# Retention and two MLPs on one core: act_b later in its step, first loads of gl and wos earlier, four p buffers, other stores and accumulators

## The chip, the core and the metric

The kernel runs on one core of a Trainium2 chip. The metric is the device time of one execution in microseconds (us). TensorE (PE) multiplies, with its weight loads shown apart as PEld; VectorE (DVE), ScalarE (ACT) and GpSimd (POOL) do the elementwise work, and SyncE (SP) issues nearly all DMA transfers. Each engine works through its own instructions in the order in which the program wrote them (the pool's scheduler is off: `manual_schedule`), and waits where an operand or a buffer isn't ready.

## The reference

Eight batches of eight heads, 576 positions, 64 wide, go through retention with one decay per head; the result, as 4608 tokens of 512, goes through two MLPs of width 2048.

```
scores = q @ k.T / 8                       # per batch and head
ret    = scores * where(i >= j, gamma[h] ** (i - j), 0)
x      = (ret @ v), laid out as tokens x 512
h = x @ w_in;   g = h * sigmoid(1.702 * h);   x = g @ w_out      # first MLP
h = x @ w_in2;  g = h - tanh(h);              out = g @ w_out2   # second MLP
```

The weights arrive as float64, seen as int64.

## The kernel before

Every operand of the large matmuls is kept as a sum of two parts, a rounded one and the rest, and a product takes three matmuls (`PASS`: 0,0; 0,1; 1,0).

**Blocks and steps.** The tokens are cut into 9 blocks of 512; the first MLP has blocks j = 0 to 8, the second j = 9 to 17, and each block has 16 steps f, one for each 128 columns of the hidden width. Step s = 16 j + f. `mm_in(s)` (L387) makes h, 12 matmuls into a PSUM tile of the pool `ps_h` (two buffers). `act_a(s)` makes t = activation(h): in the first MLP one operation on ACT (L396) and one on DVE (L397); in the second three on ACT (L401 to L403) and a chain of five on DVE (L404, L406 to L409). `g_store` (L413) writes t to DRAM.

**The lag.** The output matmuls run `LAG` = 32 steps behind: in step s the group o = s - 32. `wo_load` (L179, tile wos, three buffers, 512 KB) and `g_load` (L417, tile gl, two buffers, 256 KB) fetch weights and t for group o + 2. `act_b(o + 1)` splits gl into the two halves of g: ACT copies it (L422), DVE subtracts (L423). `mm_out(o)` (L439 where j < 9, with g as the moving side; L441 from j = 9 on, with g as the weights) adds 12 matmuls, three for each of four accumulators. After 16 groups `evac` copies the accumulators out: in the first MLP ACT into tiles o of the pool p (L449; three buffers, shared with the attention's tile p) and SP to DRAM (L450), in the second into one tile (L457, in the last block DVE's L455 too) and to the output (L459).

**What else stands in a step.** Until step 126 every second step holds an attention step (`attn_step`: L243, L257, L272, L308 on PE; L280 to L294 and L323 on DVE; L322 and L330 on ACT). The weights are decoded from float64 in 64 chunks, three pieces each (`dec_piece`: dec_a and dec_a2, dec_b, dec_c and dec_d, L104 to L140): a load stg by SP (L96), six operations on DVE and two on ACT. At the end of dec_d (L140) the 48 chunks that are not needed at once are stored to DRAM as wd (L143). Ten steps from s = 32 on hold three pieces, the later ones two. In four steps (f = 6, 8, 10, 12) of blocks j = 8 to 16 `x2_split` prepares the next block of the second MLP: ACT copies (L471), POOL subtracts (L472).

**The order in a step from s = 32 on** is the code's: mm_in(s), act_b(o + 1), attention, a decode piece, act_a(s), loads for o + 2, g_store(s - 1), mm_out(o), more decode pieces, evac at f = 15, x2_split. The first two pairs of loads and act_b(0) are issued in step 32 itself. Steps 288 to 319 hold only the output side; in the last block the accumulators are the two halves of `pat`, the attention's PSUM tile, and two tiles of `ps_h`.

Of the kernel before, what the change touches and what calls it, by code (L numbers as in the profile page):

```python
# [7 lines left out]
F32 = mybir.dt.float32  # L8
# [8 lines left out]
P = 128  # L17
# [6 lines left out]
BLK = 512  # L24
NB = NT // BLK
KD = DM // P
NF = DFF // P
# [13 lines left out]
LAG = 2 * NF  # L41
# [5 lines left out]
def kernel(  # L47
# [14 lines left out]
    wos_p = ctx.enter_context(tc.tile_pool(name="wos", bufs=3))  # L62
    x_p = ctx.enter_context(tc.tile_pool(name="x", bufs=3))
    at_p = ctx.enter_context(tc.tile_pool(name="at", bufs=2))
    p_p = ctx.enter_context(tc.tile_pool(name="p", bufs=3))
    g_p = ctx.enter_context(tc.tile_pool(name="g", bufs=2))
    t_p = ctx.enter_context(tc.tile_pool(name="t", bufs=2))
    st_p = ctx.enter_context(tc.tile_pool(name="st", bufs=2))
# [2 lines left out]
    ps_h = ctx.enter_context(tc.tile_pool(name="ps_h", bufs=2, space=bass.MemoryType.PSUM))  # L71
# [18 lines left out]
    wo_d = {}  # L90
    stg = {}
    half = {}

    def wload(m, f, c):
        t = st_p.tile([P, BLK], I64, tag="stg", name="stg", bufs=3)
# [42 lines left out]
    def dec_d(m, f, c):  # L138
        o, sv = half.pop((m, f, c))
        nc.vector.tensor_tensor(out=sv[:, 1], in0=o, in1=sv[:, 0].bitcast(F32), op=ALU.subtract)  # L140
        if (m, c) != (0, 0):
            d = dram.tile([P, 2 * DM], F32, tag=f"w{m}{f}{c}", name="wd")
            nc.sync.dma_start(out=d, in_=sv.rearrange("p a n -> p (a n)").bitcast(F32))  # L143
            (wo_d if c else w2_d)[m, f] = d
# [10 lines left out]
    def dec_piece(pieces=1):  # L155

        for _ in range(pieces):
            n, k = divmod(n_dec[0], 3)
            if n >= len(chunks) + 2:
                return  # L160
            n_dec[0] += 1
            if k == 0:
                dec_load(n + 2)
                if n >= 2:
                    dec_c(*chunks[n - 2])
                if 1 <= n <= len(chunks):
                    dec_b(*chunks[n - 1])
                continue
            if k == 1 and n >= 2:
                dec_d(*chunks[n - 2])  # L170
            if n < len(chunks):
                (dec_a if k == 1 else dec_a2)(*chunks[n])

    def wo_load(o):
        j, f = divmod(o, NF)
        if j >= 2 * NB - 2:
            return
        t = wos[o] = wos_p.tile([P, 2, DM], F32R, tag="wos", name="wos")
        nc.sync.dma_start(out=t.rearrange("p a n -> p (a n)").bitcast(F32), in_=wo_d[int(j >= NB), f])  # L179
# [43 lines left out]
    pat = ps_a.tile([P, 2, BLK], F32, name="pat")  # L223
# [148 lines left out]
    gl = {}  # L372
    gt = {}
    acc = {}
# [17 lines left out]
    def act_a(s):  # L392
        h = hps.pop(s)
        tt[s] = t = t_p.tile([P, BLK], F32, tag="t", name="t", bufs=3)
        if s < NB * NF:
            nc.scalar.activation(out=t, in_=h, func=ACTF.Tanh, scale=0.851)  # L396
            nc.vector.scalar_tensor_tensor(out=t, in0=t, scalar=1.0, in1=h, op0=ALU.add, op1=ALU.mult)  # L397
            return
        sq = t_p.tile([P, BLK], F32, tag="e", name="sq")
        pl = t_p.tile([P, BLK], F32, tag="z", name="pl", bufs=3)  # L400
        nc.scalar.activation(out=t, in_=h, func=ACTF.Tanh)  # L401
        nc.scalar.activation(out=sq, in_=h, func=ACTF.Square)  # L402
        nc.scalar.activation(out=pl, in_=sq, func=ACTF.Square, bias=abias)  # L403
        nc.vector.tensor_tensor(out=t, in0=h, in1=t, op=ALU.subtract)  # L404

        nc.vector.scalar_tensor_tensor(out=pl, in0=pl, scalar=CB, in1=sq, op0=ALU.add, op1=ALU.mult)  # L406
        nc.vector.scalar_tensor_tensor(out=pl, in0=pl, scalar=C2, in1=h, op0=ALU.mult, op1=ALU.mult)  # L407
        nc.vector.tensor_scalar(sq.bitcast(I32), sq, S_MAX, None, ALU.is_lt)
        nc.vector.copy_predicated(out=t, mask=sq.bitcast(I32), data=pl)  # L409

    def g_store(s):
        gd[s] = dram.tile([P, BLK], F32, tag=f"g{s % (LAG + NF)}", name="gd")
        nc.sync.dma_start(out=gd[s], in_=tt.pop(s))  # L413

    def g_load(s):
        t = gl[s] = t_p.tile([P, BLK], F32, tag="gl", name="gl")
        nc.sync.dma_start(out=t, in_=gd.pop(s))  # L417

    def act_b(s):
        t = gl.pop(s)  # L420
        gt[s] = g = g_p.tile([P, 2, BLK], F32R, tag="g", name="g")
        nc.scalar.activation(out=g[:, 0], in_=t, func=ACTF.Copy)  # L422
        nc.vector.tensor_tensor(out=g[:, 1], in0=t, in1=g[:, 0].bitcast(F32), op=ALU.subtract)  # L423

    def mm_out(s):
        j, f = divmod(s, NF)
        if f == 0:
            for m in range(4):
                if j < 2 * NB - 1:
                    acc[m] = ps_acc.tile([P, BLK], F32, tag=f"acc{m}", name=f"acc{m}")  # L430
                else:
                    acc[m] = pat[:, m] if m < 2 else ps_h.tile([P, BLK], F32, tag="h", name="acc")
        g, wo = gt.pop(s), wos.pop(s)
        for m in range(4):
            c = slice(m * P, (m + 1) * P)
            for n, (a, b) in enumerate(PASS):
                first, last = f == 0 and n == 0, f == NF - 1 and n == 2
                if j < NB:
                    nc.tensor.matmul(acc[m], lhsT=wo[:, a, c], rhs=g[:, b], start=first, stop=last)  # L439
                else:  # L440
                    nc.tensor.matmul(acc[m], lhsT=g[:, a, c], rhs=wo[:, b], start=first, stop=last)  # L441
# [50 lines left out]
    with tc.tile_pool(name="ps_e", bufs=RING - 1, space=bass.MemoryType.PSUM) as ps_e:  # L492

        def early(b):
            attn_early(b, ps_e.tile([P, 2, BLK], F32, tag="e", name="pe") if b % RING else pat)


        warm = g_p.tile([P, BLK], BF16, tag="g", name="warm")
        nc.gpsimd.memset(warm, 0.0)
        for _ in range(N_WARM):  # L500
            nc.tensor.matmul(pat[:, 1], lhsT=warm[:, 0:P], rhs=warm, start=True, stop=True)

        for b in range(BPB + 1):
            if b < BPT:
                for hp in (2 * b, 2 * b + 1):
                    at_scale(0, hp)
                for i in range(2):
                    for k in range(2):
                        h = 2 * (2 * b + k) + i
                        nc.scalar.activation(  # L510
                            out=mt_sb[:, b, i, k], in_=mk_sb, func=ACTF.Copy, scale=jt_sb[:, h:h + 1]
                        )
            early(b)
            dec_piece(int(b > 0))

        for f in range(NF):
            mm_in(f)
            if f < NF // 2:
                dec_piece(3)
                act_a(f)  # L520
                early(BPB + 1 + f)
            else:
                s = NF + 2 * (f - NF // 2)
                g_store(s - 1 if f > NF // 2 else f - 1)
                mm_in(s)
                dec_piece(2)
                act_a(f)
                early(BPB + 1 + f)
                dec_piece()
                act_a(s)  # L530
                g_store(f)
                mm_in(s + 1)
                dec_piece(2)
                act_a(s + 1)
                g_store(s)
            if 0 < f < NF // 2:
                g_store(f - 1)
    ps_acc = ctx.enter_context(tc.tile_pool(name="ps_acc", bufs=1, space=bass.MemoryType.PSUM))

    n_steps = 2 * NB * NF  # L540
    for s in range(LAG, n_steps + LAG):
        j, f = divmod(s, NF)
        o = s - LAG
        if o == 0:
            g_store(s - 1)
            for i in range(2):
                wo_load(i)
                g_load(i)
            act_b(0)
        if s < n_steps:  # L550
            mm_in(s)
        if s < n_steps + LAG - 1:
            act_b(o + 1)
        if s % 2 == 0 and EARLY + (s - LAG) // 2 <= TILES * BPT:
            attn_step(EARLY + (s - LAG) // 2)
        dec_piece()
        if s < n_steps:
            act_a(s)
        if s < n_steps + LAG - 2:
            wo_load(o + 2)  # L560
            g_load(o + 2)
        if o and s <= n_steps:
            g_store(s - 1)
        mm_out(o)
        dec_piece(2 if j == 2 and f < 10 else 1)
        if f == NF - 1:
            evac(o)
        if NB - 1 <= j < 2 * NB - 1:
            if f == 2:
                x2_load(j - NB + 1)  # L570
            if f in (6, 8, 10, 12):
                x2_split(j - NB + 1, (f - 6) // 2)
        if j == NB - 1:
            w2_load(f)
        if j == 2 * NB - 1:
            wo_stay(f)
# [54 lines left out]
```

## Time and profile before

| | us |
|---|---|
| median of 3 runs (lowest, highest) | 1811.34 (1808.97, 1815.0) |
| the profiled execution | 1809.77 |
| its span, first to last instruction | 1808.0 |
| PE busy in it | 1752.8 |
| DVE, ACT, POOL busy | 1070.4, 711.9, 132.7 |

The mean granted clock of PE is 0.987 of full. The profile's lines name the source line, the engine, the operation and the tiles (out<-in, buffer numbers left out); a bracket at a line's end gives the idle time ahead of it and what ended it. In the chain of waits each piece is what released the next. Matmuls are pipelined, so a row's length for several of them is a little more than the time to the next group.

### The profile page before, as it was taken

The numbers are of one execution on the slowest core, as the hardware profiler recorded it, in microseconds if no ns is written. First come the engines' busy times: TensorE is split into PE (matmuls) and PEld (weight loads), VectorE is DVE, ScalarE is ACT, GpSimd is POOL, SyncE is SP. The second block draws the span as 40 slices with busy tenths as digits, with TensorE's granted clock in tenths as the row PEclk, the third lists the DMA queues.
The fourth block names the chain that finished last, engine by engine and source line by source line (L and its number), as shares of the span: only waits on it lengthen the run. The fifth ranks groups of instructions, "written<-read, shape, count | busy, mean of one in ns | idle before, by whom it ended". The sixth has DMA issues, their size and how long they took to land.

```text
span 1808.0 us, 24474 instructions
## 1 busy us (share of the span) xinstructions
PE 1752.8 (97%) x8908; PEld 1424.1 (79%) x8908; DVE 1070.4 (59%) x1810; ACT 711.9 (39%) x1307; POOL 132.7 (7%) x111
## 2 busy tenths in 40 slices
PE   8899898999999999999999999999999999999998
PEld 5667776877778888888888888888888888888877
DVE  7887674656555333232247767767776767776622
ACT  3433333333333232222234454454445445454422
POOL 3211010101000001100000000101010100000000
PEclk9999998999999999999999999999999999999999
DMA  5656897987888666657985756575657575658733
GB/s 218 220 196 240 297 334 265 317 277 282 294 284 301 236 212 223 234 183 243 302 296 195 245 195 235 195 247 187 238 199 239 188 246 195 234 205 303 264 123 100
DMA packets 158377, 428.76 MB, mean 237 GB/s; under 512 B 17968, under 2 KB 18096, under 8 KB 152624
## 3 DMA queue, kind: packets, MB, share of 16 engines
q1 hardware_dynamic: 157680, 427.10, 69.3%
q8 instruction: 71, 1.16, 0.3%
q14 instruction: 50, 0.41, 0.1%
q10 hardware_dynamic: 576, 0.08, 0.0%
HBM read 307.57 MB, written 119.54 MB: 236 GB/s over the span
## 4 chain that ended last, share of the span: by engine, by line
PE 79%; DMA 8%; DVE 7%; ACT 2%; issue 2%; SPq 1%; ACTq 0%; DVEq 0%
PE h L387 36%; PE acc L441 20%; PE acc L439 18%; DMA gl<-gd 7%; PE pat L441 1%; PE pat L257 1%; DVE t L397 1%; DVE p L280 1%; PE pat L308 1%; DVE e L120 1%; DVE ws L140 1%; PE pat L243 1%; SPq L179 1%; ACT g L422 1%; DMA x<-o 1%
## 5 line engine op out<-in xcount | busy, mean ns | idle before, releaser
L387 PE MATMUL h<-xh,wi 128*128 128x512 f32 x2304 | 763.4, 393 | 15.0 <-DVE t L397 8.6
L387 PEld LDWEIGHTS h<-xh,wi 128*128 128x128 f32 x2304 | 434.5, 189 | 117.8 <-DVE t L397 15.9
L439 PE MATMUL acc<-g,wos 128*128 128x512 f32 x1728 | 433.1, 399 | 25.3 <-ACT o L449 15.1
L387 PE MATMUL h<-xl,wi 128*128 128x512 f32 x1152 | 450.3, 391 | 0.0
L423 DVE TENSOR_TENSOR g<-gl,g 128x512 fp32r<-128x512 f32 x288 | 198.4, 689 | 392.3 <-ACT g L422 392.1
L439 PEld LDWEIGHTS acc<-g,wos 128*128 128x128 f32 x1728 | 324.9, 191 | 104.8 <-ACT o L449 17.0
L422 ACT ACTIVATE g<-gl 128x512 fp32r<-128x512 f32 x288 | 181.9, 632 | 508.5 <-DMA gl<-gd 324.4
L441 PE MATMUL acc<-wos,g 128*128 128x512 f32 x1344 | 322.8, 389 | 0.0
L441 PEld LDWEIGHTS acc<-wos,g 128*128 128x128 f32 x1344 | 252.2, 188 | 52.4
L387 PEld LDWEIGHTS h<-xl,wi 128*128 128x128 f32 x1152 | 217.6, 189 | 44.4
L404 DVE TENSOR_TENSOR t<-h,t 128x512 f32<-128x512 f32 x144 | 99.7, 693 | 193.8 <-ACT sq L402 193.4
L401 ACT ACTIVATE t<-h 128x512 f32<-128x512 f32 x144 | 86.0, 598 | 254.6 <-PE h L387 254.5
L397 DVE SCALAR_TENSOR_TENSOR t<-t,h 128x512 f32<-128x512 f32 x144 | 98.3, 683 | 62.0 <-ACT t L396 61.8
L108 ACT ACTIVATE e<-e,ebias 128x512 int32<-128x512 int32 x64 | 46.4, 725 | 170.8 <-DVE e L106 170.8
L409 DVE COPY_PREDICATED t<-sq,pl 128x512 f32<-128x512 int32 x144 | 109.3, 759 | 4.9
L403 ACT ACTIVATE pl<-sq,abias 128x512 f32<-128x512 f32 x144 | 104.2, 724 | 4.7
L406 DVE SCALAR_TENSOR_TENSOR pl<-pl,sq 128x512 f32<-128x512 f32 x144 | 99.7, 692 | 9.2
L472 POOL TENSOR_TENSOR xl<-x2s,xh 128x512 fp32r<-128x512 f32 x36 | 46.6, 1296 | 774.1 <-ACT xh L471 774.1
L407 DVE SCALAR_TENSOR_TENSOR pl<-pl,h 128x512 f32<-128x512 f32 x144 | 98.9, 687 | 4.9
L396 ACT ACTIVATE t<-h 128x512 f32<-128x512 f32 x144 | 84.4, 586 | 37.3 <-PE h L387 36.7
L215 POOL TENSOR_TENSOR at<-at,qt_sb 128x512 f32<-128x512 f32 x35 | 46.8, 1337 | 694.8 <-DMA at<-in_attn_dram 582.8
L402 ACT ACTIVATE sq<-h 128x512 f32<-128x512 f32 x144 | 85.4, 593 | 0.0
(62 smaller groups left out, 1121.2 us busy)
## 6 DMA issues: line engine op xcount, KB each, us to landing
wos<-wd SPq DMA_DIRECT2D x256, 512.0 KB, 4.5
gd<-t SPq DMA_DIRECT2D x288, 256.0 KB, 4.4
gl<-gd SPq DMA_DIRECT2D x288, 256.0 KB, 4.4
at<-in_attn_dram SPq DMA_DIRECT2D x35, 1024.0 KB, 5.8
stg<-in_w_dram SPq DMA_DIRECT2D x64, 512.0 KB, 6.4
wd<-ws SPq DMA_DIRECT2D x48, 512.0 KB, 3.6
x<-o SPq DMA_DIRECT2D x36, 256.0 KB, 2.8
x2s<-x SPq DMA_DIRECT2D x9, 1024.0 KB, 5.7
```

The costliest lines, as they stand in the source:

```text
L387: nc.tensor.matmul(h, lhsT=win[f][:, a, k], rhs=xs[b][:, k], start=(n == 0), stop=(n == 3 * KD - 1))
L397: nc.vector.scalar_tensor_tensor(out=t, in0=t, scalar=1.0, in1=h, op0=ALU.add, op1=ALU.mult)
L401: nc.scalar.activation(out=t, in_=h, func=ACTF.Tanh)
L403: nc.scalar.activation(out=pl, in_=sq, func=ACTF.Square, bias=abias)
L404: nc.vector.tensor_tensor(out=t, in0=h, in1=t, op=ALU.subtract)
L406: nc.vector.scalar_tensor_tensor(out=pl, in0=pl, scalar=CB, in1=sq, op0=ALU.add, op1=ALU.mult)
L407: nc.vector.scalar_tensor_tensor(out=pl, in0=pl, scalar=C2, in1=h, op0=ALU.mult, op1=ALU.mult)
L409: nc.vector.copy_predicated(out=t, mask=sq.bitcast(I32), data=pl)
L422: nc.scalar.activation(out=g[:, 0], in_=t, func=ACTF.Copy)
L423: nc.vector.tensor_tensor(out=g[:, 1], in0=t, in1=g[:, 0].bitcast(F32), op=ALU.subtract)
L439: nc.tensor.matmul(acc[m], lhsT=wo[:, a, c], rhs=g[:, b], start=first, stop=last)
L441: nc.tensor.matmul(acc[m], lhsT=g[:, a, c], rhs=wo[:, b], start=first, stop=last)
```

## The change

Six edits: the pool p has four buffers; gl has three; dec_d no longer stores wd itself, but leaves it to `dec_store`, which the third decode piece of a chunk calls before its own work; the first two pairs of wo_load and g_load stand in the last two rounds of the early part and not in step 32; act_b(o + 1) stands behind act_a(s) and not ahead of the attention; and the accumulators of the last two blocks are other ones: block 16 takes the halves of `pat` for m = 0 and 1, block 17 the ordinary tiles for m = 0 and 1 and `ps_h` for the other two.

```
@@ pools @@
-    p_p = ctx.enter_context(tc.tile_pool(name="p", bufs=3))
+    p_p = ctx.enter_context(tc.tile_pool(name="p", bufs=4))
...
+    part = {}
@@ dec_d, dec_store @@
         if (m, c) != (0, 0):
+            part[m, f, c] = sv
+
+    def dec_store():
+        while part:
+            (m, f, c), sv = part.popitem()
             d = dram.tile([P, 2 * DM], F32, tag=f"w{m}{f}{c}", name="wd")
             nc.sync.dma_start(out=d, in_=sv.rearrange("p a n -> p (a n)").bitcast(F32))
             (wo_d if c else w2_d)[m, f] = d
@@ dec_piece @@
             n, k = divmod(n_dec[0], 3)
+            if k == 2:
+                dec_store()
@@ g_load @@
-        t = gl[s] = t_p.tile([P, BLK], F32, tag="gl", name="gl")
+        t = gl[s] = t_p.tile([P, BLK], F32, tag="gl", name="gl", bufs=3)
@@ mm_out @@
-                if j < 2 * NB - 1:
+                if j == 2 * NB - 2 and m < 2:
+                    acc[m] = pat[:, m]
+                elif j == 2 * NB - 1 and m > 1:
+                    acc[m] = ps_h.tile([P, BLK], F32, tag="h", name="acc")
+                else:
                     acc[m] = ps_acc.tile([P, BLK], F32, tag=f"acc{m}", name=f"acc{m}")
-                else:
-                    acc[m] = pat[:, m] if m < 2 else ps_h.tile([P, BLK], F32, tag="h", name="acc")
@@ early part, f >= 8 @@
                 g_store(s)
+                if f >= NF - 2:
+                    wo_load(f - NF + 2)
+                    g_load(f - NF + 2)
@@ steps from 32 on @@
             g_store(s - 1)
-            for i in range(2):
-                wo_load(i)
-                g_load(i)
             act_b(0)
         if s < n_steps:
             mm_in(s)
-        if s < n_steps + LAG - 1:
-            act_b(o + 1)
         if s % 2 == 0 and EARLY + (s - LAG) // 2 <= TILES * BPT:
             attn_step(EARLY + (s - LAG) // 2)
         dec_piece()
         if s < n_steps:
             act_a(s)
+        if s < n_steps + LAG - 1:
+            act_b(o + 1)
```

In the changed kernel the lines have other numbers: act_b's copy is L430, act_a's L404 (first MLP) and L409 to L411 (second), x2_split's copy L481, the attention's L330 and L338, the decode's L109 and L136, the loads L187 and L425, the stores L149 and L421.

**ACT, two steps of the first MLP with attention in the first of them.** The names: g<-gl is act_b, xh<-pat and sbd0 are the attention, e and ws the decode, t<-h is act_a. Before:

```order
L422 ACTIVATE g_3375<-gl_3345 128x512
L322 ACTIVATE xh_2701<-pat_104 128x2x128
L330 ACTIVATE sbd0_100<-s_sb0_102 64x2x64 x2
L135 ACTIVATE ws_3402<-z_3244 128x512
L396 ACTIVATE t_3406<-h_3362 128x512
L108 ACTIVATE e_3430<-e_3430,ebias_98 128x512
L422 ACTIVATE g_3448<-gl_3411 128x512
```

After:

```order
L330 ACTIVATE xh_2698<-pat_104 128x2x128
L338 ACTIVATE sbd0_100<-s_sb0_102 64x2x64 x2
L136 ACTIVATE ws_3399<-z_3242 128x512
L404 ACTIVATE t_3403<-h_3362 128x512
L430 ACTIVATE g_3406<-gl_3343 128x512
L109 ACTIVATE e_3428<-e_3428,ebias_98 128x512
```

The split of the same gl (3345 before, 3343 after) moves from ahead of the attention to behind act_a of its step; DVE's half moves with it.

**ACT, a step of the second MLP with x2_split (xh<-x2s).** Before:

```order
L401 ACTIVATE t_8715<-h_8699 128x512
L402 ACTIVATE sq_8716<-h_8699 128x512
L403 ACTIVATE pl_8717<-sq_8716,abias_99 128x512
L471 ACTIVATE xh_8562<-x2s_8560 128x512
L422 ACTIVATE g_8759<-gl_8728 128x512
```

After:

```order
L409 ACTIVATE t_8712<-h_8699 128x512
L410 ACTIVATE sq_8713<-h_8699 128x512
L411 ACTIVATE pl_8714<-sq_8713,abias_99 128x512
L430 ACTIVATE g_8723<-gl_8683 128x512
L481 ACTIVATE xh_8562<-x2s_8560 128x512
```

The copy for x2_split stood directly behind act_a; now an act_b stands between them, and it is that of the group before (gl 8683, which before the change was split ahead of L401 of this step).

**SP, the end of the early part and step 32.** stg is a chunk's load, wd its store, gd<-t g_store. Before:

```order
L413 DMA gd<-t 128x512
L143 DMA wd<-ws 128x1024
L413 DMA gd<-t 128x512 x2
L179 DMA wos<-wd 128x1024
L417 DMA gl<-gd 128x512
L179 DMA wos<-wd 128x1024
L417 DMA gl<-gd 128x512
L96 DMA stg<-in_w_dram 128x512
```

After:

```order
L421 DMA gd<-t 128x512
L187 DMA wos<-wd 128x1024
L425 DMA gl<-gd 128x512
L421 DMA gd<-t 128x512
L149 DMA wd<-ws 128x1024
L212 DMA at<-in_attn_dram 128x2048
L97 DMA stg<-in_w_dram 128x512
L421 DMA gd<-t 128x512
L149 DMA wd<-ws 128x1024
L421 DMA gd<-t 128x512
L187 DMA wos<-wd 128x1024
L425 DMA gl<-gd 128x512
```

The first pair of loads now stands a whole round earlier, the second ahead of the last g_store; the loads in the other steps keep their place behind stg.

## Rows read from the trace of the kernel before

**Rows 1.** The page, part 1: busy us (share of the span) and instructions

```profile
PE 1752.8 (97%) x8908; PEld 1424.1 (79%) x8908; DVE 1070.4 (59%) x1810; ACT 711.9 (39%) x1307; POOL 132.7 (7%) x111
```

**Rows 2.** PE's waits over the span: total us, times, longest us

```profile
PE acc L439 <- ACT o L449: 15.1, 5, 5.0
...
PE acc L439 <- ACT g L422: 9.0, 4, 5.6
```

**Rows 3.** Timeline of PE: start us, us, engine line op out<-in xcount [idle <-releaser]

```profile
185.34 5.79 PE L439 MATMUL acc<-g,wos 128*128 128x512 f32 x12 [5.61 <-ACT g L422]
...
638.71 3.01 PE L439 MATMUL acc<-g,wos 128*128 128x512 f32 x12
...
794.83 3.01 PE L439 MATMUL acc<-g,wos 128*128 128x512 f32 x12
```

**Rows 4.** Chain that ended last, in order of time: start us, us, what

```profile
237.57 8.11 DMA gl<-gd
...
247.14 0.33 DVE xl L323
...
250.37 0.61 DVE ws L140
...
253.84 6.35 DMA gl<-gd
```

**Rows 5.** SP's own waits, 180 to 600 us

```profile
SPq L143 <- DVE ws L140: 218.8, 41, 8.3
```

**Rows 6.** Timeline of ACT, end of the first block of mm_out

```profile
307.12 0.60 ACT L449 ACTIVATE o<-acc 128x512 f32<-128x512 f32 x1 [6.69 <-DMA x<-o]
```

**Rows 7.** Two stretches: us, each engine's busy time, PEclk, DMA share, GB/s

```profile
206.00:271.00 65.00, 63.49 (x382) 50.67 (x382) 48.04 (x85) 24.58 (x48) 8.25 (x6) 1.00 0.94 330
...
1412.00:1700.00 288.00, 288.00 (x1272) 238.46 (x1271) 203.03 (x319) 140.21 (x234) 14.24 (x11) 1.00 0.69 236
```

**Rows 8.** Timeline of two steps of the second MLP

```profile
1408.37 0.69 DVE L423 TENSOR_TENSOR g<-gl,g 128x512 fp32r<-128x512 f32 x1
...
1409.31 2.88 PE L441 MATMUL acc<-wos,g 128*128 128x512 f32 x12
...
1411.26 0.62 ACT L471 ACTIVATE xh<-x2s 128x512 fp32r<-128x512 f32 x1
...
1411.95 1.30 POOL L472 TENSOR_TENSOR xl<-x2s,xh 128x512 fp32r<-128x512 f32 x1 [9.58 <-ACT xh L471]
...
1412.72 0.82 DVE L408 TENSOR_SCALAR sq<-sq 128x512 int32<-128x512 f32 x1
...
1414.20 0.69 DVE L423 TENSOR_TENSOR g<-gl,g 128x512 fp32r<-128x512 f32 x1
...
1414.53 0.87 PEld L441 LDWEIGHTS acc<-wos,g 128*128 128x128 f32 x4
...
1414.75 1.52 PE L441 MATMUL acc<-wos,g 128*128 128x512 f32 x6
```

**Rows 9.** Timeline of DVE and PE where a group waited for L423

```profile
246.44 0.69 DVE L423 TENSOR_TENSOR g<-gl,g 128x512 fp32r<-128x512 f32 x1 [1.56 <-ACT g L422]
...
247.19 2.76 PE L439 MATMUL acc<-g,wos 128*128 128x512 f32 x11 [0.22 <-DVE g L423]
```

**Rows 10.** Line L408 alone: ns min/median/max

```profile
L408 DVE TENSOR_SCALAR sq<-sq x144: 419/420/867, 934.0 to 1711.9; 128x512 int32<-128x512 f32 x144
```

**Rows 11.** Timeline of ACT, two operations that wait for nothing

```profile
192.82 0.62 ACT L422 ACTIVATE g<-gl 128x512 fp32r<-128x512 f32 x1
...
193.35 0.61 ACT L135 ACTIVATE ws<-z 128x512 fp32r<-128x512 f32 x1
```

**Rows 12.** Timeline at the last mm_in's end

```profile
1711.23 5.62 PE L441 MATMUL acc<-wo,g 128*128 128x512 f32 x24
...
1713.06 0.68 DVE L423 TENSOR_TENSOR g<-gl,g 128x512 fp32r<-128x512 f32 x1
...
1719.15 9.02 PE L441 MATMUL acc<-wo,g 128*128 128x512 f32 x30 [2.30 <-ACT g L422]
```

## The prediction, made before the changed kernel ran

> **What bounds the kernel now.** I read the busy times first: TensorE (PE) is busy 1752.8 of 1808.0 us [rows 1], so nothing can be won but its 55 us of gaps and any slowing between them. Then PE's waits: most of the gap time after the start belongs to the second matmuls (L439), for the copies out of the accumulators (15.1 us in 5 waits) and for the first half of g (9.0 us in 4) [rows 2]. Then PE's own timeline, to see what the gaps cost in all. Call the 12 matmuls of mm_out(o) one group. Group 0 starts at 185.34, group 64 at 638.71, group 88 at 794.83 [rows 3]. From 64 to 88 PE has no gap: 156.12 us for 12 pairs of steps, 13.01 us a pair (one attention step in each pair). From 0 to 64 there are 32 pairs, at that pace 416.3 us; they took 453.4. So **37.1 us** are lost in the stage where weights are still being decoded, and 5.61 us more in the wait in front of group 0 [rows 3]. After group 64 nothing is left to win before the last 90 us: the waits listed are all but used up, and from 1412 to 1700 PE is busy 288.00 of 288.00 us [rows 7].
>
> Why that stage is slow: the chain of waits there runs in a circle that is not PE's [rows 4]. A load of gl takes 8.11 us (237.57), ScalarE (ACT) and VectorE (DVE) copy it to g, and only then DVE, which works in order, gets to the attention, the decode and act_a (from 247.14); the last link is L140 (250.37). SyncE (SP) waits for L140 to store wd and cannot issue the next gl load before that. One turn, two steps, is 253.84 - 237.57 = 16.27 us against 13.01. SP spends 218.8 us in 41 such waits [rows 5]. At a block's end the fourth copy out waited 6.69 us for the first one's store to land, since there are three buffers [rows 6]; PE's longest wait for a copy is 5.0 us [rows 2].
>
> **The change part by part.**
>
> 1. *The first two loads of wos and gl are issued in the last two rounds of the early part*, ahead of two or more runs of mm_in, and what they load has been stored long before. The 5.61 us in front of group 0 go. What is late next is act_b(0) itself, which now stands behind nothing that waits. **-5.6 us.**
>
> 2. *act_b(o+1) goes behind the attention, decode and act_a of its step.* The link from 247.14 to 250.37 (attention 0.33 and more, L120, L125, L397: 3.23 us) is then no longer between the load's landing and L140: the turn is 16.27 - 3.23 = 13.04 us in this slow turn, and less with a shorter load, so about the 13.01 that PE needs. The loads have more time too, since act_b may end as late as group o+1 begins. *wd's stores go one decode piece later*, so in one step of three SP issues the two loads before it waits for L140, not behind it. *The fourth buffer* takes the store's landing out of the copies. One slot of the four is still held by the attention's p tile; the copy that gets it waits for the matmuls L308 of the next step, 2.13 us (13.01 less 48 matmuls at 0.227) after mm_in, and PE needs that accumulator three groups of three matmuls, 2.04 us, later, against a copy of 0.60 [rows 6]: hidden. So I take the whole loss of this stage as the gain, **-37.1 us**, less what the DMA queues hold back.
>
> 3. *DMA in the first ten steps*, where a whole chunk is decoded in each step. A step moves wos 0.524, gl 0.262, gd 0.262, stg 0.524, wd 0.524 and a quarter of at, 0.262: 2.36 MB. From 206 to 271 us the engines moved 330 GB/s at a share of 0.94 [rows 7], so 351 GB/s would be all of it: 6.72 us a step against 6.505 of PE. Ten steps: **+2.1 us**; the bounds are 0 (the queue is ahead by then) and the rival below. The Trainium skill (SBUF — State Buffer, SBUF: two separate sides) gives about 436 GB/s as the peak of the DMA side; by that nothing would be added and the sum would be 2.1 us lower. The row speaks for the smaller figure.
>
> 4. *The price of moving act_b*, in the second MLP. act_a there is a chain of five DVE operations, and L423 follows it. The DVE order stays what it was, but the L423 behind act_a(s) now makes g for the group that comes next (o+1), not for the one after it. In a plain step it ends at 1408.37 + 0.69 = 1409.06, and the group starts at 1409.31 [rows 8]. PE asks for this half of g at the weight load of the third matmul (j >= 9: the load starts one matmul, 0.227 us, ahead: 1414.53 for the matmul of 1414.75), or with the second matmul's load where g is the moving side (groups below 144). A wait ends 0.06 us after L423 (247.13 to 247.19) [rows 9]. The margins are 1409.54 - 1409.12 = 0.42 us, and 0.19 us below group 144: plain steps **cost nothing**.
>  In four steps of each block ACT also makes xh (L471) and GpSimd (POOL) xl (L472, 1.30 us). There L408 takes 0.82 us and not its median of 0.42 [rows 8, 10]: it ends at 1413.54, 0.29 us after POOL's 1413.25, so it waits for POOL. The blocks j = 9 to 16 have four such steps each: 32 collisions. The change puts L422 ahead of L471 on ACT, and an operation behind L422 starts 0.53 us after it (192.82 to 193.35) [rows 11]. So L471 starts at 1411.79, POOL at 1412.48, still before L408 can (1412.72), and POOL's end, L408, L409 and L423 come 0.53 us later: L423 ends at 1415.42, PE may go on at 1415.48. The third matmul's load was due at 1414.98 and its matmul at 1415.20; a held load costs 0.11 us more (11 matmuls in 2.76 us [rows 9] for 11 x 0.227 and the 0.16 that the last one of a full group of 2.88 [rows 8] shows beyond its 12). Lost: 0.28 + 0.11 = 0.39 us in the 24 steps from group 144 on; for the second matmul, due at 1414.98, 0.50 + 0.11 = 0.61 us in the 8 before. 24 x 0.39 + 8 x 0.61 = **+14.3 us**. Bounds: 0, if L408 gets in first, and 32 x 0.61 = 19.5.
>
> 5. *The end.* At s = 288 no mm_in stands between two groups. Group 256 starts at 1711.23; L423 for it now comes behind act_a(287), at 1713.06, and ends at 1713.74 [rows 12]. PE stops before its third matmul (1711.68) until 1713.80 and loses 2.2 us, which it had free before: it waited 2.30 us at 1719.15 for gl of group 258, whose load stands behind the output's stores, and these come about 0.6 us later with the copies. The two overlap: **+0.6 us**, bounds -2.3 (no wait left) and +2.8 (both in full; the 30 matmuls behind the wait took 9.02 us where 6.8 is usual, so a second slow stretch of 2.2 is in this). The accumulators in pat keep group 256 from waiting for copies that now come after act_b; no wait for them was there, so nothing is gained.
>
> 6. The third gl buffer frees the slot a step earlier; nobody waits for it in the stage with gaps. The other stores' shift in the early part lies behind loads that are two chunks ahead: nothing.
>
> Sum: -5.6 - 37.1 + 2.1 + 14.3 + 0.6 = **-25.7 us**. The profiled run took 1809.77 us (span 1808.0 and 1.8 around it) and would take 1784.1; the median of the three runs is 1.6 above it: 1811.34 - 25.7 = **1785.6**.
>
> **The rivals.**
> *POOL loses the race.* L408 needs to start 0.24 us earlier, or L471 to come that much later, and POOL would be the one that waits: no 14.3. For it: a quarter of a microsecond is little. Against it: POOL starts 0.07 us behind L471's end (1411.26 + 0.62 = 1411.88, then 1411.95 [rows 8]), and L408 cannot start before L407 is done. 1785.6 - 14.3 = 1771.3. The Trainium skill (SBUF — State Buffer, Who interferes with whom) says the pair of ports of the two engines is locked for a whole operation and that the order of issue decides who blocks; by that rule the 0.24 us are all that stands between the two results. The rows agree as far as they show one side of it.
>
> *The queues, not the circle, hold the decode stage.* After the ten steps, DMA still has 2.0 MB a step, 309 of 351 GB/s, for some 48 steps; if the landing times grow with it, the circle closes at 13.04 or more with each slow load and only half of the 37.1 comes back: 1785.6 + 18.5 = 1804.1. For it: a share of 0.94 [rows 7]; against it: a landing may now be late by several us before PE feels it.
>
> *Every step of the second MLP waits (slower than before).* The margins of 0.42 and 0.19 us are thin. If the DVE chain is longer by x in all 144 steps, PE loses 24 (x - 0.19) + 88 (x - 0.42) + 32 x. At 0.46 us this eats the 25.7; at 0.6, less than one more DVE operation (0.69), it costs 45: 1831. Against it: these operations and their order don't change, and the wait for L422 becomes earlier.
>
> **How the numbers follow.** Forecast as worked out, 0.66 (its own range 1778 to 1793, from the bounds of the DMA, collision and end terms); POOL loses 0.14; queues 0.12; slower 0.08. The range of 8 in 10 reaches from 1769 (the first rival without the DMA term) to 1804 (the second). A difference under 0.3% (5.4 us) can't be told from none here. Faster by more: 0.66 + 0.14 + two thirds of the queues' case, 0.08, is 0.88; the same, 0.04; slower 0.08.
>
> **What would show it.** In the changed profile: group 0 with no wait in front; group 64 some 41 us earlier; no wait for the copies out in the first MLP; SP's waits for L140 hardly shorter but harmless. In 32 steps of the second MLP L408 at about 1.36 us, and PE's weight loads waiting for L423 some 0.5 us each. Two short gaps at the end in place of one. Wrong would be: waits of PE for L423 in plain steps, L408 at 0.42 us everywhere, or gaps that remain before group 64.

## The result, and the profile after

The changed kernel takes **1787.88 us** (median of 4 runs, 1787.29 to 1789.52) against 1811.55 (4 runs) of the kernel before on the same chip: a ratio of 0.987, 95% interval 0.9852 to 0.9887. It was forecast faster at 1785.6, and it came out 2.3 us above that. The profiled execution took 1788.14 us, its span is 1786.3. What follows goes by spans: 1808.0 - 1786.3 = 21.7 us.

The page's busy times, to be read beside [rows 1]; the columns are the same:

```profile
PE 1747.3 (98%) x8908; PEld 1413.9 (79%) x8908; DVE 1078.4 (60%) x1810; ACT 696.1 (39%) x1307; POOL 133.6 (7%) x111
```

The same instructions, 5.5 us less of PE's busy time and 16.2 us less of its gaps. The granted clock averages 0.997 of full over the span and averaged 0.987 before. PE's waits over the span, to be read beside [rows 2] (total us, times, longest):

```profile
PE h L395 <- DVE wi L141: 8.2, 7, 2.5
PE h L395 <- DVE t L405: 6.3, 6, 1.7
PE acc L449 <- DVE g L431: 4.4, 14, 0.5
...
PE pat L451 <- DVE g L431: 1.9, 1, 1.9
PE acc L449 <- ACT g L430: 1.8, 1, 1.8
...
PE pat L451 <- ACT g L430: 0.9, 1, 0.9
```

The 15.1 us for copies out of the accumulators are gone, and of the 9.0 us for g one wait of 1.8 is left. Where the time went is read from the starts of the groups. These are the rows that answer to [rows 3], on PE's timeline (start us, us, what; the lengths are cut by the windows asked for):

```profile
182.18 3.01 PE L449 MATMUL acc<-g,wos 128*128 128x512 f32 x12
...
604.11 2.11 PE L449 MATMUL acc<-g,wos 128*128 128x512 f32 x8
...
1672.06 2.20 PE L451 MATMUL acc<-wos,g 128*128 128x512 f32 x9
```

and the last of them in the kernel before:

```profile
1692.19 1.98 PE L441 MATMUL acc<-wos,g 128*128 128x512 f32 x8
```

| stretch | before, us | after, us | gain |
|---|---|---|---|
| start to group 0 | 185.34 | 182.18 | 3.16 |
| group 0 to 64, decoding and attention | 453.37 | 421.93 | 31.44 |
| group 64 to 252, both MLPs in full run | 1053.48 | 1067.95 | -14.47 |
| group 252 to the end | 115.81 | 114.24 | 1.57 |
| span | 1808.0 | 1786.3 | 21.7 |

So the gain of the decode stage is large and 14.5 us of it are given back later, in a part of the kernel that had no gaps before. Group 64 starts 34.6 us earlier, where some 41 were forecast.

**The decode stage.** What the gain consists of can be read from the whole stretch from group 0 to 64, first before and then after (windows: us, busy times of PE, PEld, DVE, ACT, POOL, PEclk, DMA share, GB/s):

```profile
185.34:638.71 453.37, 431.06 (x2417) 346.17 (x2417) 267.34 (x489) 154.33 (x313) 38.79 (x30) 0.97 0.83 287
```

```profile
182.18:604.11 421.93, 418.15 (x2418) 340.54 (x2416) 262.08 (x488) 155.83 (x314) 40.02 (x31) 1.00 0.88 313
```

PE's gaps fall from 22.3 to 3.8 us. Its busy time for the same matmuls falls from 431.06 to 418.15 us, with a granted clock (PEclk) of 0.97 before and 1.00 after. So of the 31.4 us 18.5 are gaps, and 12.9 are matmuls that ran slower before. Part of the second belongs to the early loads: group 0 took 5.79 us behind its wait [rows 3] and takes 3.01 now.

The rows that answer to [rows 4], in the chain of the changed kernel:

```profile
223.98 9.59 DMA gl<-gd
...
234.31 0.69 DVE g L431
235.00 0.60 DVE ws L141
```

A load of 9.59 us, longer than the 8.11 before, lands; act_b's half on DVE follows, and L141 directly behind it. The attention, L121, L126 and L405, 3.23 us in the old chain, no longer stand between. SP's waits for L141, over the same 180 to 600 us, fall from 218.8 us in 41 [rows 5] to

```profile
SPq L149 <- DVE ws L141: 89.6, 25, 6.8
```

In their place SP waits longer for the attention's matmuls ahead of the loads of at: 92.4 us in 16, where it was 19.1 in 8.

The stretch of [rows 7] now moves more in the same 65 us:

```profile
206.00:271.00 65.00, 64.42 (x391) 52.35 (x390) 49.13 (x95) 27.31 (x54) 4.89 (x5) 1.00 0.98 355
```

355 GB/s at a share of 0.98: the DMA engines have next to no idle time, and PE is busy for 64.42 us all the same.

**The second MLP.** A step with x2_split in the changed kernel, to be read beside the last five rows of [rows 8]:

```profile
1398.08 0.62 ACT L430 ACTIVATE g<-gl 128x512 fp32r<-128x512 f32 x1
...
1398.61 0.61 ACT L481 ACTIVATE xh<-x2s 128x512 fp32r<-128x512 f32 x1
...
1399.30 1.28 POOL L482 TENSOR_TENSOR xl<-x2s,xh 128x512 fp32r<-128x512 f32 x1 [9.99 <-ACT xh L481]
1399.54 1.32 DVE L416 TENSOR_SCALAR sq<-sq 128x512 int32<-128x512 f32 x1
...
1401.56 0.67 DVE L431 TENSOR_TENSOR g<-gl,g 128x512 fp32r<-128x512 f32 x1
1401.58 2.12 PE L451 MATMUL acc<-wos,g 128*128 128x512 f32 x7
...
1402.28 1.22 PEld L451 LDWEIGHTS acc<-wos,g 128*128 128x128 f32 x6 [0.51 <-DVE g L431]
```

The copy L481 starts 0.53 us behind L430, GpSimd (POOL) 0.69 us behind that, and L416, which takes 0.42 us alone, takes 1.32: it ends at 1400.86, 0.28 us after POOL's 1400.58. L431 ends at 1402.23, the weight load of the third matmul goes on at 1402.28, 0.51 us late. PE's weight loads over the stretch from group 64 on show how often (606 to 1720 us):

```profile
PEld acc L451 <- DVE g L431: 12.4, 24, 0.6
PEld acc L449 <- DVE g L431: 5.9, 8, 0.7
```

24 and 8, the counts of the forecast; the plain steps don't appear. The starts of the groups give the price: 9.50 us more than before from group 144 to 252 and 4.97 from 64 to 144, so 0.40 us for each of the 24 and 0.62 for each of the 8.

### The profile page after: what moved, and what is told of

It is laid out like the page before. It is cut to its first block, busy times and chain, and to the rows that moved or that the text cites. A ratio compares the mean times of both kernels' runs of the same rounds, so it can differ in the third digit from the quotient of the medians.

```text
span 1786.3 us, 24630 instructions
## 1 busy us (share of the span) xinstructions
PE 1747.3 (98%) x8908; PEld 1413.9 (79%) x8908; DVE 1078.4 (60%) x1810; ACT 696.1 (39%) x1307; POOL 133.6 (7%) x111
## 4 chain that ended last, share of the span: by engine, by line
PE 74%; DVE 12%; DMA 6%; ACT 5%; issue 3%; SPq 1%; ACTq 0%; DVEq 0%; POOL 0%
PE h L395 33%; PE acc L449 18%; PE acc L451 17%; DMA gl<-gd 3%; DVE sq L416 2%; DVE g L431 2%; PE pat L265 2%; ACT pl L411 1%; DVE pl L414 1%; DVE pl L415 1%; ACT t L409 1%; PE pat L316 1%; PE pat L451 1%; PE pat L251 1%; ACT sq L410 1%
## 5 line engine op out<-in xcount | busy, mean ns | idle before, releaser
L449 PE MATMUL acc<-g,wos 128*128 128x512 f32 x1728 | 428.0, 395 | 6.3 <-DVE g L431 4.4
L449 PEld LDWEIGHTS acc<-g,wos 128*128 128x128 f32 x1728 | 320.8, 188 | 85.5 <-DVE g L431 10.4
L451 PE MATMUL acc<-wos,g 128*128 128x512 f32 x1344 | 330.1, 392 | 2.2
L431 DVE TENSOR_TENSOR g<-gl,g 128x512 fp32r<-128x512 f32 x288 | 197.1, 685 | 114.6 <-ACT g L430 114.6
L409 ACT ACTIVATE t<-h 128x512 f32<-128x512 f32 x144 | 86.1, 598 | 424.1 <-PE h L395 424.1
L430 ACT ACTIVATE g<-gl 128x512 fp32r<-128x512 f32 x288 | 179.5, 623 | 130.2 <-DMA gl<-gd 76.6
L405 DVE SCALAR_TENSOR_TENSOR t<-t,h 128x512 f32<-128x512 f32 x144 | 98.5, 684 | 162.5 <-ACT t L404 162.0
L404 ACT ACTIVATE t<-h 128x512 f32<-128x512 f32 x144 | 84.8, 589 | 141.8 <-PE h L395 141.2
L331 DVE TENSOR_TENSOR xl<-pat,xh 128x256 fp32r<-128x256 f32 x56 | 23.7, 423 | 161.2 <-ACT xh L330 161.2
L109 ACT ACTIVATE e<-e,ebias 128x512 int32<-128x512 int32 x64 | 46.4, 724 | 169.5 <-DVE e L107 169.5
L411 ACT ACTIVATE pl<-sq,abias 128x512 f32<-128x512 f32 x144 | 104.2, 724 | 4.7
L415 DVE SCALAR_TENSOR_TENSOR pl<-pl,h 128x512 f32<-128x512 f32 x144 | 98.9, 687 | 4.9
```

## The experiments

Twelve kernels. The stretches in the table are read from the traces, one profiled execution each, in the way of the table above; a ratio is to the kernel before on the same chip. The medians of that kernel on the chips of these runs were 1810.98 to 1812.97 us, so a difference of 2 us between medians of two rows can be the chip's. The profiled executions of e10 (1782.72 us) and e3 (1776.54) lie 5 and 4 us below their medians, so the stretches read from them can be that much too short.

| kernel | median us | ratio to before (95%) | 0 to 16 | 16 to 64 | 64 to 252 |
|---|---|---|---|---|---|
| before | 1811.55 | | 114.2 | 339.2 | 1053.48 |
| changed | 1787.88 | 0.9870 (0.9852 to 0.9887) | 106.4 | 315.5 | 1067.95 |
| e1_split_first | 1772.68 | 0.9766 (0.9747 to 0.9784) | 106.9 | 315.1 | 1054.35 |
| e2_split_dve | 1771.92 | 0.9761 (0.9741 to 0.9780) | 105.8 | 316.5 | 1053.49 |
| e3_act_b_back | 1780.78 | 0.9806 (0.9784 to 0.9828) | 114.8 | 310.7 | 1053.48 |
| e9_act_b_alone | 1798.90 | 0.9906 (0.9884 to 0.9929) | 107.1 | 317.8 | 1068.02 |
| e10_store_later_alone | 1787.83 | 0.9878 (0.9848 to 0.9908) | 108.9 | 317.3 | 1053.48 |
| e11_p_four_alone | 1805.51 | 0.9970 (0.9953 to 0.9987) | 113.4 | 334.4 | 1053.49 |
| e4_store_at_once | 1788.36 | 0.9863 (0.9848 to 0.9879) | 107.4 | 314.9 | 1067.98 |
| e5_p_three | 1789.29 | 0.9867 (0.9852 to 0.9882) | 106.2 | 317.3 | 1068.24 |
| e6_p_five | 1784.42 | 0.9832 (0.9810 to 0.9853) | 107.0 | 311.2 | 1068.05 |
| e8_loads_back | 1793.53 | 0.9890 (0.9874 to 0.9906) | 106.2 | 313.3 | 1068.01 |
| e7_tail | 1786.14 | 0.9861 (0.9835 to 0.9887) | 106.8 | 315.7 | 1067.92 |
| best_dve | 1764.94 | 0.9748 (0.9723 to 0.9773) | 107.0 | 311.4 | 1053.49 |

### Where the 14.5 us of the second MLP come from

Theory: a later POOL operation holds L416 in 32 steps. Rival: act_b at the end of a long DVE chain makes PE wait a little in every step.

**e1_split_first** moves the ACT copy of x2_split ahead of act_b:

```
             act_a(s)
+        if NB - 1 <= j < 2 * NB - 1 and f in (6, 8, 10, 12):
+            x2_split(j - NB + 1, (f - 6) // 2)
         if s < n_steps + LAG - 1:
             act_b(o + 1)
...
-            if f in (6, 8, 10, 12):
-                x2_split(j - NB + 1, (f - 6) // 2)
```

> The changed kernel with one thing altered: in the steps with x2_split its ACT copy (L481) stands ahead of act_b again, so that GpSimd starts some 0.53 us earlier, as before the change; act_b stays behind act_a. Theory (the 14.5 us lost between group 64 and group 252 come from the 32 steps in which L416 waits for a later GpSimd operation): the loss goes, about 1787.9 - 14.4 = 1773.5 us, L416 at most 0.87 us, PE's weight loads wait for L431 in next to no step. Rival (the loss comes from act_b standing at the end of the DVE chain in every step, with thin margins): between 1786 and 1789 us.

**e2_split_dve** takes POOL out of it:

```
-        nc.gpsimd.tensor_tensor(out=lo[:, k], in0=t[:, k], ...)
+        nc.vector.tensor_tensor(out=lo[:, k], in0=t[:, k], ...)
```

> The changed kernel with x2_split's subtraction on DVE in place of GpSimd (36 operations of about 0.69 us more on DVE, behind act_b in its order). Theory (GpSimd's operation is what holds L416): L416 is 0.42 us in all 144 steps and nothing is lost from group 64 on, about 1773 us, the same as with the copy moved ahead. Rival (the DVE chain is too long as such): more DVE work makes it worse, 1788 to 1800 us.

Measured: 1772.68 and 1771.92 us, 15 and 16 less than the changed kernel, as the theory said of both. Line L416 alone in the changed kernel, in e1 and in e2 (ns min/median/max):

```profile
L416 DVE TENSOR_SCALAR sq<-sq x144: 418/420/1384, 899.4 to 1691.8; 128x512 int32<-128x512 f32 x144
```

```profile
L416 DVE TENSOR_SCALAR sq<-sq x144: 419/421/871, 897.7 to 1676.5; 128x512 int32<-128x512 f32 x144
```

```profile
L416 DVE TENSOR_SCALAR sq<-sq x144: 419/420/422, 897.9 to 1675.8; 128x512 int32<-128x512 f32 x144
```

In e1 L416 still waits for POOL in the 32 steps, but no longer than in the kernel before, and PE's weight loads from 606 to 1660 us wait for L431 no more than

```profile
PEld acc L449 <- DVE g L431: 1.8, 8, 0.2
```

In e2 it waits nowhere, and 36 more DVE operations of 0.69 us cost nothing: groups 64 to 252 take 1053.49 us, to 0.01 what they took before the change. The rival falls, since act_b stands in the same place in both. The Trainium skill (SBUF — State Buffer, Who interferes with whom) says that where a DVE operation contends with GpSimd, whichever is issued first has the ports that they share for its whole instruction and the other waits. The end of L416 0.28 us behind POOL's in the rows above agrees. That the length of L416 moves with POOL's start, and is 0.42 us without POOL, is what e1 (up to 0.87), the changed kernel (up to 1.38) and e2 (0.42) show.

### Which edit opened the decode stage

Theory: the move of act_b did. Rival: the other edits did, and the move only costs.

**e3_act_b_back** is the changed kernel with that one edit undone; **e9_act_b_alone** is the kernel before with that one edit:

```
         if s < n_steps:
             act_a(s)
+        if s < n_steps + LAG - 1:
+            act_b(o + 1)
```

> The changed kernel with act_b(o+1) back ahead of the attention and act_a; all other edits stay. Theory (moving act_b is what opened the circle of waits in the decode stage, and it alone costs in the second MLP): the decode stage loses 20 to 30 us again, the 14.4 us of the second MLP come back: 1793 to 1805 us. Rival (the later wd stores, the fourth buffer and the early loads made the gain, act_b only costs): 1787.9 - 14.4 = 1773.5 us.

> The kernel before with the one edit that act_b(o+1) stands behind act_a. Theory: some 20 to 28 us of the decode stage's loss go, 14.4 us are lost in the second MLP: 1798 to 1806 us. Rival (the other edits made the gain): 1811.5 + 14.4 = 1826 us.

Neither side had it. The move alone is worth 28.5 us from group 0 to 64 (453.4 to 424.8) and 1798.9 us, as the theory said. But without it the other edits are worth 27.8 (425.5) and the kernel is *faster* than the changed one, 1780.78 us, 12 us under the theory's range. So each of two edits opens the circle. In the trace e3 loses 8.4 us from 0 to 16 against the changed kernel and wins 4.8 from 16 to 64: its pair of steps behind the third block's end takes 13.30 us, and the changed kernel's 17.34 (below, at e6). Against e1 and e2, where act_b is moved and the collision is gone, e3 is 8 to 9 us slower, so the move is worth that much once its price isn't paid. The next experiments look for the other edit.

**e10_store_later_alone** puts `dec_store` and its call into the kernel before, **e11_p_four_alone** the fourth buffer of p:

```
             n, k = divmod(n_dec[0], 3)
+            if k == 2:
+                dec_store()
```

```
-    p_p = ctx.enter_context(tc.tile_pool(name="p", bufs=3))
+    p_p = ctx.enter_context(tc.tile_pool(name="p", bufs=4))
```

> The kernel before with the one edit that wd is stored one decode piece later (dec_store). With act_b back in its place the changed kernel still kept 27.9 of 31.5 us between groups 0 and 64, nearly all of it after group 16, so one of the other edits opens the circle too. Theory 1 (the stores: from step 42 on one step in three no longer waits for L140 ahead of its loads): groups 0 to 16 as slow as before, some 15 to 20 us of the stretch from 16 to 64 won, none in the rest: 1793 to 1798 us. Theory 2 (the fourth p buffer did it): within 4 us of the kernel before, 1809 to 1813 us.

> The kernel before with the one edit of four buffers in the pool p. Theory 1 (the later stores open the circle): only the waits for copies go, 15.1 us at most with what the clock adds: 1800 to 1808 us, gaps for gl remain. Theory 2 (this buffer did it): 1785 to 1793 us.

The store's delay by one decode piece alone gives **1787.83 us, as much as the whole change** (1787.88). The fourth buffer alone gives 5.5 us. In its profiled run they are no gaps: between groups 0 and 64 PE's idle time is 22.2 us (22.3 before), and its busy time falls from 431.1 to 425.6 us, at a granted clock of 0.99. Of the two theories the first holds, with a gain above its range: from 16 to 64 the 339.2 us become 317.3. It missed the first block, which was to stay as slow and took 5.2 us less. What it does can be seen in what ACT waits for, 180 to 600 us, in the kernel before, in e10 and in the changed kernel:

```profile
ACT g L422 <- DMA gl<-gd: 150.4, 42, 7.7
```

```profile
ACT g L430 <- DMA gl<-gd: 131.8, 50, 8.0
```

```profile
ACT g L430 <- DMA gl<-gd: 56.3, 25, 5.5
```

With the store later act_b still waits for its loads for nearly as long as before, but hardly any of it reaches PE: in e10 PE's waits for ACT's half of g are 6.2 us in 2, of which 5.9 are the one in front of group 0, and those for copies out are 7.2 us in 5, where they were 15.1. SP's waits for L141 go from 218.8 to 138.0 us. With act_b moved as well act_b's own waits shrink to little over a third.

**e4_store_at_once** is the changed kernel with the store in its old place:

```
             part[m, f, c] = sv
+            dec_store()
...
-            if k == 2:
-                dec_store()
```

> The changed kernel with wd's store issued by dec_d itself again, ahead of the next two loads in one step of three. Theory (with act_b moved the loads have time to spare): within 3 us of the changed kernel, 1788 to 1791 us. Rival (the later stores are what opened the circle): 10 us or more are lost, over 1798 us.

1788.36 us: once act_b is moved, the store's place is worth nothing. So the two edits do the same thing twice, as far as the whole time shows. What the move still adds stands in the column from 0 to 16, where the first ten steps hold three pieces each and the store keeps its place ahead of the loads, delayed or not: 105.8 to 107.4 us in the ten kernels with act_b moved, 108.9 to 114.8 in the four without.

### The smaller edits

**e5_p_three** is the changed kernel with `bufs=3` for p again, **e6_p_five** has five, and to make room two for gl:

```
-    p_p = ctx.enter_context(tc.tile_pool(name="p", bufs=4))
+    p_p = ctx.enter_context(tc.tile_pool(name="p", bufs=5))
...
-        t = gl[s] = t_p.tile([P, BLK], F32, tag="gl", name="gl", bufs=3)
+        t = gl[s] = t_p.tile([P, BLK], F32, tag="gl", name="gl")
```

> The changed kernel with three buffers in the pool p again. Theory: at the ends of blocks 0 to 5 the last copies wait for stores again, 3 to 5 us in some of them: 1791 to 1800 us. Rival (the copies were late only because ACT was held by act_b's wait for gl): as the changed kernel, 1787 to 1789 us.

> The changed kernel with five buffers in the pool p and, to make room, two for gl. In the changed kernel's trace the attention's multiply L288 behind the third block's end waits 2.31 us for the store of a copy whose slot it takes, and the group after it (o = 49) starts late. With five slots the p tile takes the slot of the p tile before. Theory: no such wait, about 4.6 us less, 1783 to 1784 us; and the third gl buffer was not needed. Rival (the third gl buffer carries part of the gain): over 1789 us.

e5 can't be told from the changed kernel (1789.29, 0.3 above its rival's range). The rival's reason is only part of it. In e5, 180 to 620 us, the copies still wait for stores as long as in the kernel before (11.9 us in 3), but little of it reaches PE (15.1 us in 5 before):

```profile
ACT o L459 <- DMA x<-o: 11.0, 4, 3.7
```

```profile
PE acc L449 <- ACT o L459: 4.5, 3, 2.7
```

The longest of these, 2.7 us, stands behind the end of the third block, where the pair of steps takes 17.66 us. The changed kernel has no wait for a copy there, and its pair takes 17.34 us all the same, for another reason. e6 is 3.5 us faster (the intervals just touch; 4.6 less was expected), and its trace shows where from. In the changed kernel, behind the end of the third block:

```profile
500.76 0.69 DVE L288 TENSOR_TENSOR p<-pat,mt_sb 128x512 f32<-128x512 f32 x1 [2.31 <-DMA x<-o]
...
504.58 0.50 PE L449 MATMUL acc<-g,wos 128*128 128x512 f32 x1 [1.85 <-ACT g L430]
505.39 4.38 PE L449 MATMUL acc<-g,wos 128*128 128x512 f32 x11 [0.30 <-DVE g L431]
```

The attention's multiply writes a p tile, which takes the slot of the first copy out and waits for its store; DVE stands, act_a and act_b come late, PE waits 1.85 us and then runs 11 matmuls in 4.38 us where 2.65 is usual. The pair of steps takes 17.34 us and not 13.01. In e6 L288 never waits for a store, this pair takes 13.71 us, and groups 16 to 64 take 311.2. So the fourth buffer took away the copy's wait there and put the p tile's in its place; the fifth takes away both. The third gl buffer, gone there, was not needed.

**e8_loads_back** puts the first two pairs of loads back into step 32:

```
             g_store(s - 1)
+            for i in range(2):
+                wo_load(i)
+                g_load(i)
             act_b(0)
```

> The changed kernel with the first two pairs of loads back in step 32. Theory: PE waits in front of group 0 again, 5 to 6 us: 1793 to 1794 us. Rival (the stage behind has slack that takes it up): 1787 to 1789 us.

1793.53 us, 5.65 more, inside the theory's range: the wait in front of group 0 is back, 5.8 us. In the profiled run groups 0 to 64 take 2.5 us less than in the changed kernel (419.4), so that the spans differ by 4.2; whether the stage takes up part of the wait isn't shown.

**e7_tail** puts act_b(256) ahead of act_a(287) and loads gl one group further ahead from there on:

```
+        if s == n_steps - 1:
+            act_b(o + 1)
         if s < n_steps:
             act_a(s)
...
+        if n_steps - 1 <= s < n_steps + LAG - 3:
+            g_load(o + 3)
```

> The changed kernel with another end: in step 287 act_b(256) stands ahead of act_a(287) again, and from there on gl is loaded one group further ahead, so that the load for group 258 stands in front of the output's stores. Theory (PE loses 1.87 us for L431 and 0.93 us for gl there, and some to the clock behind them): 2.5 to 5 us less, 1783 to 1785.5 us. Rival (the end is set by something else): 1787 to 1789 us.

1786.14 us, 1.7 less, which the intervals don't separate from the changed kernel. In the trace group 252 to the end takes 112.3 us and not 114.2, so the waits do go down, but by less than expected: the load for group 259 now stands behind the output's stores in place of 258's, and PE waits for that one:

```profile
PE pat L451 <- ACT g L430: 1.6, 1, 1.6
```

### A version that beats both

**best_dve** is e2, e6 and e7 together.

> The changed kernel with x2_split's subtraction on DVE, five p buffers with two for gl, and the other end. Theory (the three losses are apart and add up): 1771.9 - 3.5 - 3.5 = 1765 us, 1763 to 1767. Rival (they overlap, or two gl buffers cost where act_b's slack is used up): 1769 to 1773 us.

**1764.94 us** (1764.19 to 1766.06), a ratio of 0.9748 (0.9723 to 0.9773) to the kernel before: 46.0 us less, and 22.9 less than the changed kernel. The losses were apart and add up: the three alone gave 16.0, 3.5 and 1.7 us, 21.2 in all. Of the 23.4 us between the two spans 2.5 lie ahead of group 0, where the start varies from run to run (next section). PE's waits from 180 to 1000 us are all but gone:

```profile
PE acc L449 <- DVE g L431: 1.3, 5, 0.3
PE acc L449 <- ACT o L459: 0.6, 2, 0.3
```

A kernel with the later store, five p buffers and act_b in its old place was not run.

## Why the prediction was right, and where it was not

*The sum.* Forecast -25.7, measured -21.7 by spans and -23.7 by medians. The terms, as the prediction numbered them:

1. **Early loads, -5.6: right.** The wait is gone, and without them the median is 5.65 us longer (e8). Group 0 came only 3.16 us earlier because the early part itself was longer in this run, by 2.4 us already at 85.89 us (83.47 before), where the two programs still have the same instructions in the same order: in the kernels that share the early loads group 0 starts between 179.73 (best_dve) and 182.18.

2. **The decode stage, -37.1, and 3. the queues, +2.1: right in direction, 3.6 us too much.** 31.4 came. 4.3 us of what is missing are the one slow pair of steps behind the third block. The step that failed there is the one on the fourth buffer: it followed the copy that takes the p tile's slot and called the conflict hidden, and it did not follow the p tile that takes a copy's slot, which waits for a store. e6 took that wait away. The term for the queues came out in size: groups 0 to 10 took 66.4 us where five pairs at 13.01 take 65.1, so 1.3 for the forecast 2.1. That the queues are what costs the 1.3 isn't shown: PE's waits there are 0.5 us in 2, for L431. The rival in which the queues keep half of the gain fell; the loads of gl take 7.4 to 10.2 us there and act_b has the time. The prediction took the whole loss as one thing, the circle; 12.9 us of what came are matmuls at a lower clock, which no step of it follows.
 **The reason was only half right.** The text gave the move of act_b as what opens the circle, and the store's delay a line. The delay alone does nearly as much as the move alone (27.1 and 28.5 us from group 0 to 64 in the profiled runs, e10's perhaps a few us too good). With the delay in place the move wins some 8 us in the first block, gives 4.8 back up to group 64 and pays 14.5 in the second MLP (e3). And SP's waits for L141 were to be hardly shorter; they fell to less than half.

4. **The collisions, +14.3: right**, in size (14.47), in number (24 and 8), in price (0.40 and 0.62 us for 0.39 and 0.61) and in cause (e1, e2). Its own factors give 14.2. L416 was to take about 1.36 us and takes 1.32 in the rows shown. The rival in which POOL loses the race did not come about, and neither did the one in which every step waits.

5. **The end, +0.6: near, but the profile hides it.** By the table 1.57 us were won there. The two gaps are there (1.87 and 0.93 us, 2.8 for the 2.30 before), but the matmuls behind them keep their pace. In the kernel before, 30 matmuls took 9.02 us behind the gap [rows 12]; in the changed one the six behind the second gap are

```profile
1699.81 1.92 PE L451 MATMUL pat<-wo,g 128*128 128x512 f32 x6 [0.93 <-ACT g L430]
...
1701.57 1.54 PE L451 MATMUL acc<-wo,g 128*128 128x512 f32 x6
```

 0.40 us longer than usual (1.52), and the next are as usual. The granted clock over 20 us around these places is 0.91 before and 1.00 after:

```profile
1709.00:1729.00 20.00, 17.70 (x70) 13.76 (x69) 6.55 (x10) 6.51 (x12) 0.00 (x0) 0.91 0.52 162
```

```profile
1688.00:1708.00 20.00, 17.20 (x74) 13.20 (x73) 7.23 (x12) 7.32 (x13) 0.00 (x0) 1.00 0.58 184
```

 The edits don't decide this. e10, whose end is the same program as the kernel before's, waits 2.43 us at the same place and keeps its clock; e6, with the changed kernel's order, loses it behind a gap of 1.87 us. The 20 us around this place in e10 and in e6:

```profile
1684.00:1704.00 20.00, 17.57 (x77) 13.84 (x76) 6.90 (x11) 7.05 (x13) 0.00 (x0) 1.00 0.54 173
```

```profile
1683.50:1703.50 20.00, 17.67 (x69) 13.37 (x68) 6.93 (x11) 7.32 (x13) 0.00 (x0) 0.91 0.58 184
```

 Where the clock held, group 252 to the end takes 113.8 us with the old end (e10) and 114.2 with the new one (changed): the change costs some 0.4 us, near the forecast 0.6. That 1.57 us were won in the profiled runs is chance: the clock fell at the end of the one and not of the other. What makes it fall stays open. The accumulators were not tried alone; e9, which has act_b moved but the old accumulators and gl buffers, takes 114.7 us there.

That the sum came so near is in part luck: by spans the early part came out 2.4 us and the decode stage 3.6 short of the forecast, and the end 2.2 better than it. The lower end of its own range, 1778, doesn't follow from the bounds that it names: with the collisions at nothing they give 1766, and with the collisions as forecast 1781.

## What to carry to other kernels

When a stage is held by a circle of waits through several engines, list every edit that cuts it and try each alone: here a store moved by one piece, behind the loads in its queue, gave by itself as much as the whole change, and with it in place the larger move cost more than it added until its price in a later stage was found and taken away. When an operation is moved to the end of an engine's chain, look in the stages that had no gap too, and follow what is queued behind it on *each* engine: half a microsecond on ACT became half a microsecond on POOL, on DVE and then on PE, 32 times. Before a difference in one stretch is put down to an edit, compare the granted clock there: the same end took 115.8 us in one kernel's profile and 113.8 in another's. And where tiles of two kinds share a pool, follow both directions, the old tile that holds a new one's slot and the new one that waits for an old one's store.

## What the runs showed of the hardware

A DVE operation of 0.42 us with one input (L416) that meets a running POOL operation ended 0.28 to 0.29 us after POOL's end, whether that made it 0.82 to 0.87 us long (before, e1) or 1.32 to 1.38 (changed), 32 times in each. Not every DVE operation is held: in e1 L415 starts 0.10 to 0.16 us behind the same POOL operation and takes its usual 0.69 us. The subtraction L431, whose two inputs both lie in SBUF, took 1.36 to 1.37 us in place of 0.69 in the four steps of e1 where it met POOL in this way.

DMA sustained 355 GB/s at a share of 0.98 over 65 us, more than the 351 that the kernel before let one estimate, with PE busy for 64.42 of the 65.

The granted clock fell behind a gap of 1.87 us in e6 and held behind one of 2.43 us in e10, so the length of one gap didn't decide it here.

The stretch from group 64 to 252 took 1053.48 or 1053.49 us in six kernels: where PE had no gap, the traces repeat to a hundredth of a microsecond, and a loss of 0.4 us in 32 steps stands out at once.
